# Accumulations of the first layer's two GEMMs emitted in four pieces each, with attention steps between the pieces; front order searched anew

## The chip, the cores and the metric

The program runs on one core of one Trainium2 chip. Its time is the device time of one execution in microseconds (us); of several runs the median counts. The engines are TensorE (PE: matmuls and transposes; PEld is its weight load), VectorE (DVE), ScalarE (ACT), GpSimd (POOL) and SyncE (SP, which here only issues DMAs). Each engine works through its instructions in the order in which the kernel emits them, and an instruction waits until what it reads is written and what it overwrites is read.

## What is computed

```python
# attention: q, k, v are (2, 8, 576, 64); heads 0-3 see the last 32 positions,
# heads 4-7 every fourth of the last 128
scores = where(mask, q @ k.T / 8, -1e9);  attn = softmax(scores);  a = attn @ v
x = a.transpose(0, 2, 1, 3).reshape(1152, 512)
# first layer (moe_*, w_in 512 x 1024, w_out 1024 x 512)
h = x @ w_in;  solu = h * softmax(h)
ln = (solu - mean(solu)) / sqrt(var(solu) + 1e-6) * g_ln
x = ln @ w_out
# second layer (moe2_*, four experts, w1 512 x 1024, w2 1024 x 512)
out = sum_e p[:, e] * (relu(x @ w1[e]) @ w2[e])
```

The first layer's weights come as float64 and are turned into float32 on the chip, by bit operations. Every GEMM is done in three products of rounded halves (high by high, high by low, low by high), so each operand is first split into a high and a low part.

## The kernel before

The front of the kernel (attention and the first layer) and the first eighth of the second layer are written as generators, each a chain of short steps, and the string ORDER says in which order the steps are emitted. A name in ORDER means the next step of that generator; the loop at the end of `fused_kernel` calls `next` on it. A plus behind a name sets `alt`, which moves that step's work to another engine: a copy (`copy`) from ACT to DVE, an addition or subtraction (`pick`) from DVE to POOL, or the other way round for `poolv`. A star and a number behind a name would set `fill`, the number of extra bf16 matmuls that `busy` emits; no entry has a star. As each engine keeps the emitted order, a step that waits holds up what stands behind it on its engine, and nothing else.

The names, in which b is the batch half and t a third of its 576 positions:

- `lI.j`, `lO.j.t`, `lD.u.b`, `lP.t.b`, `lvd.b`, `lvp.t.b`, `lW.g`, `lV.g`: loads, all on SP's queue. lP and lD bring q and k of the plain and the dilated heads, lI w_in, lO w_out, lvp and lvd v, lW and lV the second layer's weights.
- `AP.t.b`, `AD.u.b`: q, then k are transposed on PE into a PSUM pair and copied to SBUF; steps 1 and 3 are PE's, 2 and 4 the copies.
- `UP.t.b`, `UD.t.b`: one of twelve attention units in twelve steps: scores on PE (1), maximum, subtraction (DVE: 2, 3), exponential (ACT: 4), sum, reciprocal (DVE: 5, 6), product (DVE, or POOL with a plus: 7), transposes (PE: 8), copy (9), values (PE: 10), high part (11) and low part (12) of x.
- `VI.j`: w_in's rows 128 j and on, in seven steps: two on ACT, two on DVE, an addition, the high part, the low part; j = 0 and 4 are the two halves of the first 128 rows. `VO.j.t`: w_out's rows 256 j + 128 t and on, also seven steps, scaled by g_ln.
- `H.t`: the first GEMM for 128 positions. Its 24 matmuls (four k blocks, three products, two halves of the 1024 columns) go into one PSUM pair `pm`; then maximum (DVE), exponential (ACT), product with h and its sum (DVE), centring (DVE or ACT).
- `T.t`: eight transposes of H.t's result, its square's sum (ACT), high and low part.
- `X.c.dp`: the second GEMM for 384 positions and half of the output columns, 48 matmuls into one pair `pm`, then one copy. X.c needs T of three tiles.
- `WP.g`, `WV.g`, `XQ.s`: operands of the second layer (weights and x; its products follow a scheme with seven instead of eight block products); `u.s` and `d.t` are its two GEMMs for the first group g = 0. `endE`, `endA`, `endH`, `endX` free memory, `misc` and `sc` are small.

H.t needs the attention units that cover its positions: of the plain heads (k blocks 0 and 1) those of its 192 positions, of the dilated heads (k blocks 2 and 3) two or three units, since these run over every fourth position. So H.0 needs UP.0.0, UD.0.0 and UD.1.0, and H.1 needs UP.0.0, UP.1.0 and all three UD of the first half.

There are two PSUM pairs under the name `pm` and two under `pa`. `pm` serves AD, the first half's AP, H, X and every second product of the second layer; `pa` serves the rest. A step that takes a pair waits until the last reader of the pair two before it is done: for H that is the product's step, for X the copy.

A step of H, as it is emitted (L380 to L388):

```python
for kk in range(KD):
    ...
    for i, (xx, ww, n) in enumerate(seq):
        nc.tensor.matmul(pm[:, n, :], ...)
yield
```

From the second group of the second layer on (g = 1 to 7, from 260 us) plain loops set the order.

Of the kernel before, what the change touches and what calls it, by code (L numbers as in the profile page):

```python
# [21 lines left out]
ORDER = """
lI.0 VI.0 lI.3 VI.0 lP.0.0 lD.1.0 AP.0.0 AP.0.0 VI.0 AD.1.0 VI.3 VI.3 lI.4 VI.3 AP.0.0 VI.3 VI.4 VI.4 lD.0.0 VI.3 AP.0.0 lP.1.0 lI.1 UP.0.0 AD.1.0
VI.3+ AD.1.0 UP.0.0 AD.0.0 AD.1.0 VI.4 AD.0.0 AD.0.0 UP.0.0 AP.1.0 AD.0.0 UP.0.0 lD.0.1 VI.0 VI.3+ AP.1.0 lvp.0.0 lI.2 UD.0.0 AP.1.0 UD.1.0 lvd.0 VI.4
VI.4 VI.0+ UD.0.0 UD.0.0 UD.0.0 UD.2.0 UD.1.0 VI.1 VI.0 UP.0.0 UD.1.0 UP.0.0 lP.2.0 UD.2.0 UD.0.0 UD.0.0 UP.0.0+ VI.0+ UP.0.0 VI.4 UD.1.0 UD.0.0+ VI.1
lO.0.1 UD.1.0 AP.1.0 UD.2.0 UD.1.0 UP.0.0 VI.1 UP.0.0 UD.2.0 VI.1 UD.1.0+ UD.2.0 UP.0.0+ UP.0.0 VI.2 UD.0.0 UD.0.0+ AD.0.1 UP.1.0 UD.1.0 VI.4+ UP.1.0
AD.0.1+ VI.2 lO.0.0 lP.0.1 UD.2.0 VI.2 UP.1.0 UD.0.0 UD.1.0 VI.2 AD.0.1 lvp.1.0 VI.2 lD.1.1 UD.0.0 VI.1+ UD.1.0 VI.1 AD.0.1+ UP.1.0 UD.1.0 VI.2 VI.1+
UP.1.0 UD.1.0 VO.0.0 VI.2 VO.0.1 AP.2.0 VO.0.0 UD.2.0+ UD.0.0 AP.2.0 H.0 UP.1.0 UP.1.0+ H.0 VO.0.0 AP.2.0 VO.0.1 UP.1.0 UD.2.0 VO.0.0 H.0 UP.1.0 misc
UD.2.0 UP.1.0 AP.0.1 H.0 VO.0.0+ UP.1.0+ AD.1.1 UP.1.0 VO.0.1 AP.2.0 AP.0.1 VO.0.1 UP.2.0 UP.2.0 VO.0.1+ lO.1.0 UD.2.0 AD.1.1 UD.2.0 lvp.2.0 AD.1.1
UP.2.0 endE lP.1.1 UD.2.0 VO.0.0 AD.1.1 VO.1.0 VO.0.0 UP.2.0 VO.1.0 H.0 VO.0.1 H.1 UP.2.0 VO.1.0 VO.1.0 UP.2.0 VO.1.0 AP.0.1 H.1 AP.0.1 UP.2.0+ T.0  # L30
UP.2.0 VO.0.1 H.1 T.0 T.0+ lO.1.1 H.1 T.0 lO.2.0 H.1 VO.1.1 VO.1.1 UP.2.0 H.2 AP.1.1 VO.1.1 UP.2.0 VO.1.1 VO.2.0 H.2 VO.1.1+ AP.1.1 UP.2.0 UP.2.0 H.2
UD.0.1 UD.0.1 VO.1.0 UP.0.1 UD.0.1 UP.0.1 VO.1.0 UD.0.1 UD.0.1 UD.0.1 lO.2.1 H.2 UD.0.1+ T.1 T.1 UP.0.1 VO.1.1 VO.2.0 VO.2.0 lvd.1 H.3 VO.2.1 VO.1.1
lvp.0.1 T.1 VO.2.0 VO.2.1 T.1 AP.1.1 VO.2.1 UP.0.1 VO.2.1 UD.0.1 AP.1.1 UD.1.1 UP.0.1 UP.0.1 UD.1.1 UD.0.1 VO.2.0+ VO.2.0 UD.0.1 UD.0.1 UD.1.1 UD.0.1
lP.2.1 AP.2.1 UD.1.1 lO.3.0 UP.0.1+ AP.2.1 lvp.2.1 UP.0.1 UD.1.1 H.2 UD.2.1 UP.0.1 UD.1.1 UP.0.1 UD.1.1+ UD.2.1 UD.2.1 UP.0.1 VO.2.1+ UP.0.1 AP.2.1
AP.2.1+ UD.1.1 VO.3.0 UD.2.1 UD.1.1 T.2 UD.1.1 lO.3.1 H.3 VO.2.1 UD.1.1 UD.2.1 T.2 UD.2.1 VO.2.0 VO.2.1 UD.1.1 T.2+ H.4 VO.3.1 T.2 VO.3.0 VO.3.1 VO.3.0
UD.2.1+ VO.3.1 VO.3.0 UP.1.1 UP.1.1 VO.3.0+ UD.2.1 H.3 UD.2.1 UP.1.1 VO.3.0 UP.2.1 H.3 VO.3.1 UP.1.1 UP.1.1 VO.3.1 VO.3.0 VO.3.1 VO.3.1 UD.2.1 UD.2.1
H.3+ UP.1.1 X.0.1 UP.1.1+ UP.2.1 UP.2.1 lvp.1.1 UP.1.1 H.4 UP.2.1 UP.2.1 UP.2.1 H.4 UD.2.1 UP.2.1 UP.2.1 H.4 UP.1.1+ UP.1.1 UP.2.1 UP.2.1 UP.2.1 endA
UP.1.1 X.0.1 X.0.0 H.5 UP.1.1 X.0.0+ T.3 T.3 H.5 T.3 H.6 H.5 H.4+ UP.2.1 T.4 T.4 H.5 H.6 T.3 T.4+ H.6 H.5 H.7 H.6 T.5 T.5 H.8 H.7 H.7 H.6+ T.4 H.7 T.6
# [715 lines left out]
```

## Time and profile before

| | us |
|---|---|
| median of three runs | 561.86 (561.75 to 563.1) |
| the profiled execution | 561.9 |
| its span | 560.1 |
| PE busy | 533.2 (95%) |
| DVE busy | 365.1 (65%) |
| ACT busy | 197.5 (35%) |
| POOL busy | 191.6 (34%) |

The span runs from the first to the last instruction of one profiled execution. An engine's busy time is the time in which it has an instruction in work; neighbouring instructions of one engine can overlap by some tens of ns, so the sum of their durations can be a little more than the busy time. The rest is idle time; where the profile knows what ended a wait, it names it behind an arrow.

### The profile page before, as it was taken

To read this page: it belongs to the slowest core of one execution; us is meant where nothing else is said; L and a number is where in the kernel's file an instruction comes from. 1 tells how busy PE (TensorE), PEld (TensorE's weight loads), DVE (VectorE), ACT (ScalarE), POOL (GpSimd) and SP (SyncE) were. 2 spreads that over 40 slices of the span, in tenths; PEclk is the share of its full clock that TensorE was granted. 3 is DMA by queue.
4 is the path that set the end of the run, shared out by engine and by line. 5 is a ranking of instruction groups with operands and counts; after the bars stand their busy time and mean duration, and the time that the engine had idled before them with its cause. 6 is when DMAs were issued, how large, how long until landed. Compare 5 with 4: busy or idle time off the path is not lost.

```text
span 560.1 us, 9023 instructions
## 1 busy us (share of the span) xinstructions
PE 533.2 (95%) x3772; PEld 479.6 (86%) x3772; DVE 365.1 (65%) x472; ACT 197.5 (35%) x309; POOL 191.6 (34%) x143
## 2 busy tenths in 40 slices
...
DMA packets 33944, 35.79 MB, mean 64 GB/s; under 512 B 18800, under 2 KB 21872, under 8 KB 33520
## 3 DMA queue, kind: packets, MB, share of 16 engines
...
q14 instruction: 11, 0.09, 0.1%
...
## 4 chain that ended last, share of the span: by engine, by line
PE 84%; DVE 8%; ACT 3%; issue 2%; DMA 1%; SPq 1%; DVEq 0%; ACTq 0%
PE pa L615 18%; PE pm L615 17%; PE pm L545 15%; PE pa L545 15%; PE pm L386 9%; PE pm L433 6%; PE pa L357 2%; DMA draw<-in_moe_w_in_dram 1%; PE pa L413 1%; DVE xol L464 1%; PE pa L343 1%; PE pa L318 1%; DVE hl L464 1%; ACT pt L184 1%; DVE cva L206 1%
## 5 line engine op out<-in xcount | busy, mean ns | idle before, releaser
L558 DVE SCALAR_TENSOR_TENSOR hl<-ct,hh 128x512 fp32r<-128x512 f32 (+1 forms) x64 | 63.2, 1005 | 33.3 <-ACT hh L556 33.2
L556 ACT ACTIVATE hh<-ct 128x512 fp32r<-128x512 f32 (+1 forms) x64 | 42.2, 682 | 59.7 <-DVE ct L588 29.7
L545 PE MATMUL pm<-xoh,hh 128*128 128x256 f32 (+1 forms) x192 | 56.9, 296 | 1.1 <-DVE ct L588 1.1
L615 PE MATMUL pm<-wh,hh 128*128 128x512 f32 (+1 forms) x148 | 56.9, 384 | 0.6 <-DVE xf L620 0.6
L545 PE MATMUL pm<-xol,hh 128*128 128x256 f32 (+1 forms) x192 | 56.9, 297 | 0.3 <-DVE xol L464 0.3
L545 PE MATMUL pa<-xoh,hh 128*128 128x256 f32 (+1 forms) x192 | 56.9, 296 | 0.0
L545 PE MATMUL pa<-xoh,hl 128*128 128x256 f32 (+1 forms) x192 | 56.8, 296 | 0.0
L545 PE MATMUL pm<-xoh,hl 128*128 128x256 f32 (+1 forms) x192 | 56.8, 296 | 0.0
L545 PE MATMUL pa<-xol,hh 128*128 128x256 f32 (+1 forms) x192 | 56.8, 296 | 0.0
L615 PE MATMUL pm<-wl,hh 128*128 128x512 f32 (+1 forms) x148 | 56.8, 384 | 0.0
L615 PE MATMUL pm<-wh,hl 128*128 128x512 f32 (+1 forms) x148 | 56.7, 383 | 0.0
L615 PE MATMUL pa<-wh,hh 128*128 128x512 f32 x144 | 56.2, 390 | 0.1
L615 PE MATMUL pa<-wl,hh 128*128 128x512 f32 x144 | 56.1, 390 | 0.0
L615 PE MATMUL pa<-wh,hl 128*128 128x512 f32 x144 | 56.0, 389 | 0.0
L464 POOL TENSOR_TENSOR wl<-wl,wh 128x1024 fp32r<-128x1024 f32 x8 | 19.3, 2412 | 96.6 <-ACT wh L184 95.4
L620 DVE SCALAR_TENSOR_TENSOR xf<-pm,pr,xf 128x512 f32<-128x512 f32 (+1 forms) x33 | 24.1, 730 | 32.9 <-PE pm L615 32.9
L620 DVE SCALAR_TENSOR_TENSOR xf<-pa,pr,xf 128x512 f32<-128x512 f32 x31 | 23.1, 745 | 29.4 <-PE pa L615 29.4
L184 ACT CAST wh<-wl 128x1024 fp32r<-128x1024 f32 x15 | 15.8, 1053 | 71.0 <-PE pa L615 40.6
L464 POOL TENSOR_TENSOR hl<-sw,hh 128x512 fp32r<-128x512 f32 x20 | 30.4, 1520 | 27.8 <-ACT hh L184 27.8
L545 PEld LDWEIGHTS pm<-xoh,hh 128*128 128x128 f32 x192 | 36.4, 190 | 1.6 <-issue 1.3
L572 POOL TENSOR_TENSOR ct<-ct,ct 128x512 f32<-128x512 f32 (+1 forms) x15 | 22.3, 1484 | 45.0 <-ACT ct L570 45.0
L545 PEld LDWEIGHTS pm<-xol,hh 128*128 128x128 f32 x192 | 36.4, 190 | 0.8 <-DVE xol L464 0.5
...
## 6 DMA issues: line engine op xcount, KB each, us to landing
...
```

The costliest lines, as they stand in the source:

```text
L184: nc.scalar.copy(out, in_)
L206: pick().tensor_tensor(out=au, in0=au, in1=low.bitcast(U32), op=ALU.add)
L357: nc.tensor.matmul(po[64 * row:64 * row + 64, 0, o:o + 96], lhsT=vv, rhs=pt[:, j, :, g, :], start=True, stop=True)
L386: nc.tensor.matmul(pm[:, n, :], lhsT=xx[:, kk, cols], rhs=ww["in", kk][:, 512 * n:512 * n + 512], start=(kk == 0 and i < 2), stop=(kk == K ...
L433: nc.tensor.matmul(pm[:, dd, 0:CW], lhsT=w_, rhs=x_[:, f, :], start=(f == 0 and i == 0), stop=(f == KF - 1 and i == 2))
L464: pick().tensor_tensor(out=out, in0=a, in1=b, op=op)
L545: nc.tensor.matmul(ps[:, ff, 0:n], lhsT=a[:, kk, fc], rhs=b[:, kk, :], start=kk == 0 and m == 0, stop=kk == 1 and m == 2)
L556: nc.scalar.activation(out=hv, in_=src, func=AF.Relu)
L558: nc.vector.scalar_tensor_tensor(out=lv, in0=src, scalar=0.0, in1=hv.bitcast(F32), op0=ALU.max, op1=ALU.subtract)
L572: poolv().tensor_tensor(out=c12, in0=c21, in1=c22, op=ALU.add)
L615: nc.tensor.matmul(po[:, u, 0:dn], lhsT=h_[:, f, cols], rhs=w_, start=(f == 0 and i == 0), stop=(f == 3 and i == 2))
L620: nc.vector.scalar_tensor_tensor(out=acc[:, t, dc], in0=po[:, u, 0:dn], scalar=pr[:, t, e:e + 1], in1=acc[:, t, dc], op0=ALU.mult, op1=ALU ...
```

## The change

H.t yields after each of its four k blocks, and X.c.dp after each pair of f blocks, with both halves of its output columns in turn; so each is emitted in four pieces of 6 or 12 matmuls, and ORDER names an H eight times instead of five and an X five times instead of twice. The number of matmuls and the operands are the same. `KORD` is the order of H's k blocks, which is as before. The tile `warmb`, `busy`, `fill` and the four calls of `busy` are gone.

ORDER is new as a whole. It differs from the old one in the sequence of steps and in which steps have a plus. Of the additions and subtractions in the front, the old order gives POOL 11 of 12 products of attention, 4 of 5 low parts of w_in and 2 of 5 additions there, and 6 of 8 additions for w_out; the new one 7, 1, 3 and 7. The old order's head and the new order's head, its part around the end of attention and its part around the start of the second layer:

```diff
 ORDER = """
-lI.0 VI.0 lI.3 VI.0 lP.0.0 lD.1.0 AP.0.0 AP.0.0 VI.0 AD.1.0 VI.3 VI.3 lI.4 VI.3 AP.0.0 VI.3 VI.4 VI.4 lD.0.0 VI.3 AP.0.0 lP.1.0 lI.1 UP.0.0 AD.1.0
-VI.3+ AD.1.0 UP.0.0 AD.0.0 AD.1.0 VI.4 AD.0.0 AD.0.0 UP.0.0 AP.1.0 AD.0.0 UP.0.0 lD.0.1 VI.0 VI.3+ AP.1.0 lvp.0.0 lI.2 UD.0.0 AP.1.0 UD.1.0 lvd.0 VI.4
-VI.4 VI.0+ UD.0.0 UD.0.0 UD.0.0 UD.2.0 UD.1.0 VI.1 VI.0 UP.0.0 UD.1.0 UP.0.0 lP.2.0 UD.2.0 UD.0.0 UD.0.0 UP.0.0+ VI.0+ UP.0.0 VI.4 UD.1.0 UD.0.0+ VI.1
-lO.0.1 UD.1.0 AP.1.0 UD.2.0 UD.1.0 UP.0.0 VI.1 UP.0.0 UD.2.0 VI.1 UD.1.0+ UD.2.0 UP.0.0+ UP.0.0 VI.2 UD.0.0 UD.0.0+ AD.0.1 UP.1.0 UD.1.0 VI.4+ UP.1.0
-AD.0.1+ VI.2 lO.0.0 lP.0.1 UD.2.0 VI.2 UP.1.0 UD.0.0 UD.1.0 VI.2 AD.0.1 lvp.1.0 VI.2 lD.1.1 UD.0.0 VI.1+ UD.1.0 VI.1 AD.0.1+ UP.1.0 UD.1.0 VI.2 VI.1+
-UP.1.0 UD.1.0 VO.0.0 VI.2 VO.0.1 AP.2.0 VO.0.0 UD.2.0+ UD.0.0 AP.2.0 H.0 UP.1.0 UP.1.0+ H.0 VO.0.0 AP.2.0 VO.0.1 UP.1.0 UD.2.0 VO.0.0 H.0 UP.1.0 misc
-UD.2.0 UP.1.0 AP.0.1 H.0 VO.0.0+ UP.1.0+ AD.1.1 UP.1.0 VO.0.1 AP.2.0 AP.0.1 VO.0.1 UP.2.0 UP.2.0 VO.0.1+ lO.1.0 UD.2.0 AD.1.1 UD.2.0 lvp.2.0 AD.1.1
-...
+lP.0.0 AP.0.0 lI.0 VI.0 AP.0.0+ AP.0.0 VI.0 lI.3 AP.0.0+ UP.0.0 lD.1.0 VI.3 VI.3 lD.0.0 VI.3 AD.1.0 UP.0.0 lI.4 UP.0.0 VI.0 lP.1.0 AD.0.0 lI.1 AD.1.0
+lI.2 VI.3 AD.1.0 VI.3 VI.3 AD.1.0 AD.0.0+ VI.4 VI.4 AD.0.0 VI.0 lP.2.0 AD.0.0+ VI.3 VI.4 VI.4 VI.0+ AP.1.0 UD.0.0 VI.0+ lvp.0.0 lD.0.1 AP.1.0 UP.0.0
+VI.4+ UD.0.0 UD.1.0 VI.4 UD.0.0 UD.0.0 UP.0.0 UD.0.0 UD.0.0 lvd.0 VI.1 VI.1 UD.0.0+ UD.1.0 UD.2.0 lO.0.0 UD.1.0 VI.4 AP.1.0 UD.2.0 VI.1 misc AP.1.0
+UP.0.0 VI.1 VI.2 UD.0.0 UD.1.0 UD.2.0 VI.0 VI.2 UP.0.0 UP.0.0 UD.1.0 UD.0.0 UD.1.0 lvp.1.0 UP.0.0 UP.1.0 AP.2.0 UP.0.0 UD.1.0 VI.1 VI.1 VI.2 AD.0.1
+UP.0.0 lD.1.1 VI.2 AP.2.0 UP.1.0 UP.1.0 lO.0.1 AD.0.1 UP.0.0 AP.2.0 UD.1.0 UP.1.0 lP.0.1 VI.2+ AD.0.1 UP.1.0 UD.0.0 AP.2.0+ H.0 UD.1.0 VI.2 VI.2+
+UD.2.0 UD.0.0+ UD.0.0 UD.1.0 VI.1 UP.1.0 UD.1.0+ UD.2.0 UD.1.0 UP.2.0 H.0 H.0 AD.0.1 VO.0.0 UD.2.0 UD.2.0 VO.0.0 UP.2.0 H.0 UP.1.0+ UP.2.0 UP.2.0
+UP.1.0 VO.0.0 H.0 UD.2.0 UP.1.0 UP.1.0 H.0 VO.0.0 UP.1.0+ UD.2.0 AD.1.1 H.0 AD.1.1 UP.2.0 VO.0.1 UP.1.0 lP.1.1 UD.2.0 AD.1.1 endE VO.0.1 UD.2.0+ H.1
+UD.2.0 H.0 UP.2.0 AD.1.1 H.1 VO.0.0+ UP.2.0+ VO.0.1 AP.0.1 VO.0.0 VO.0.1 T.0 AP.0.1 VO.0.0 T.0 T.0 VO.0.1+ UD.0.1 UD.0.1 UD.0.1 T.0 VO.0.1 H.1 H.1
+...
+UP.1.1 UP.2.1 VO.2.0+ VO.2.1 X.0.1 H.4 VO.2.1 H.4 VO.2.1 lvp.2.1 UP.1.1 H.4 UP.1.1 lO.3.0 VO.3.0 UP.2.1 UD.2.1 UD.2.1+ VO.2.0 VO.2.0 UP.1.1 VO.2.1+
+UP.2.1 lO.3.1 VO.2.1 VO.2.1 VO.3.1 VO.3.1 X.0.1 UP.1.1 UP.1.1 X.0.0 UP.1.1 VO.3.1 UD.2.1 VO.3.0 VO.3.1 X.0.0 X.0.1 VO.3.0 VO.3.0 UP.2.1 VO.3.0+ UD.2.1
+UP.2.1 VO.3.1 lvp.1.1 X.0.0 UD.2.1 VO.3.0 VO.3.1 VO.3.0 UP.1.1 VO.3.1 UP.2.1 H.3 X.0.1 UP.1.1+ UP.2.1+ UP.1.1 UP.2.1 UP.1.1+ endA X.0.1 X.0.0 UP.1.1
+H.5 X.0.0+ H.6 H.5 T.3 T.3 H.5 H.4 H.5 H.5 H.5 H.6 T.3+ T.4 H.5 T.3 T.4 H.6 H.6 H.7 H.7 H.7 H.5 T.5 H.6 H.6 H.6 T.4 T.5 H.6+ H.7 H.8 H.7 H.8 H.7 H.8
+T.4 T.6 T.5 H.7 H.7+ T.6 T.5 H.8 H.8 T.6+ X.1.1 H.8 X.1.1 H.8 X.1.0 X.1.1 H.8 T.6 T.7 T.8 T.8 T.7 X.1.1 X.1.1+ X.1.0 X.1.0 X.1.0 T.7 endH T.7 lW.0
+WP.0+ T.8 T.8 X.2.0 WP.0 sc WP.0 X.1.0 WP.0 WP.0+ WP.0 WP.0 WP.0 XQ.0 X.2.1 XQ.0 WP.0 X.2.0 WP.0 XQ.0 XQ.0 XQ.0+ WP.0+ X.2.0 WP.0 XQ.0 X.2.0 X.2.1
+XQ.0+ X.2.1 XQ.0 X.2.0 X.2.1 XQ.0+ WP.0 XQ.0 XQ.0 endX XQ.0+ XQ.0 WP.0+ XQ.0+ WP.0 WP.0+ XQ.1+ X.2.1+ WP.0 XQ.0 XQ.1 WP.0+ XQ.0 XQ.1 u.0 u.0 XQ.1 u.0
+...
 """
```

The rest of the diff:

```diff
+KORD = (0, 1, 2, 3)
-    warmb = ap1.tile([128, 224], BF16, name="warmb", tag="warmb")
-    nc.vector.memset(warmb, 0.0)
 ...
-    fill = [0]
-    def busy(ps):
-        for _ in range(fill[0]):
-            nc.tensor.matmul(ps[:, 1, 288:512], lhsT=warmb[:, 0:128], rhs=warmb, start=True, stop=True)
 ...
-            busy(pa)
 ...
-            busy(pa)
 ...
-        busy(ps)
 ...
-        busy(po)
 ...
     def moe_H(t):
         pm = psm.tile([128, 2, 512], F32, name="pm", tag="pm")
         cols = slice(128 * t, 128 * t + 128)
-        for kk in range(KD):
+        for n_, kk in enumerate(KORD):
             seq = [(xhi, whi, n) for n in range(2)] + [(xhi, wlo, n) for n in range(2)] + [(xlo, whi, n) for n in range(2)]
             for i, (xx, ww, n) in enumerate(seq):
                 nc.tensor.matmul(pm[:, n, :], lhsT=xx[:, kk, cols], rhs=ww["in", kk][:, 512 * n:512 * n + 512],
-                                 start=(kk == 0 and i < 2), stop=(kk == KD - 1 and i >= 4))
-        yield
+                                 start=(n_ == 0 and i < 2), stop=(n_ == KD - 1 and i >= 4))
+            yield
         e = ep.tile([128, 2, 512], F32, name="e", tag="e")
         nc.vector.tensor_reduce(out=nmx[:, t:t + 1], in_=pm, axis=AX.XY, op=ALU.max, negate=True)
         yield
 ...
     def moe_X(c, dp):
         lh, ll = hts["ln", c]
         pm = psm.tile([128, 2, 512], F32, name="pm", tag="pm")
-        for dd in range(2):
-            d = 2 * dp + dd
-            for f in range(KF):
-                o = (f % 2) * 512 + d * 128
-                wh = whi["out", f // 2][:, o:o + 128]
-                wl = wlo["out", f // 2][:, o:o + 128]
-                for i, (w_, x_) in enumerate(((wh, lh), (wh, ll), (wl, lh))):
-                    nc.tensor.matmul(pm[:, dd, 0:CW], lhsT=w_, rhs=x_[:, f, :], start=(f == 0 and i == 0), stop=(f == KF - 1 and i == 2))
-        yield
+        for j in range(KF // 2):
+            for f in (2 * j, 2 * j + 1):
+                for dd in range(2):
+                    d = 2 * dp + dd
+                    o = (f % 2) * 512 + d * 128
+                    wh = whi["out", j][:, o:o + 128]
+                    wl = wlo["out", j][:, o:o + 128]
+                    for i, (w_, x_) in enumerate(((wh, lh), (wh, ll), (wl, lh))):
+                        nc.tensor.matmul(pm[:, dd, 0:CW], lhsT=w_, rhs=x_[:, f, :], start=(f == 0 and i == 0), stop=(f == KF - 1 and i == 2))
+            yield
         copy(xf[0].rearrange("p (k n) -> p k n", k=KD)[:, 2 * dp:2 * dp + 2, c * CW:c * CW + CW], pm[:, :, 0:CW])
     xf = []
 ...
-        fill[0] = int(n or 0)
```

## Rows read from the trace of the kernel before

**Rows 1.** the page's head and engine part (busy us, share, instructions)

```profile
span 560.1 us, 9023 instructions
...
PE 533.2 (95%) x3772; PEld 479.6 (86%) x3772; DVE 365.1 (65%) x472; ACT 197.5 (35%) x309; POOL 191.6 (34%) x143
```

**Rows 2.** stretches of the span: length, then each engine's busy time (x instructions)

```profile
12.34:39.68 27.34, 21.04 (x370) 16.70 (x369) 24.98 (x37) 16.36 (x26) 13.58 (x10) 1.00 0.96 259
39.68:53.12 13.44, 11.74 (x143) 9.88 (x144) 10.17 (x17) 8.70 (x15) 6.66 (x5) 1.00 0.38 75
53.12:70.30 17.18, 16.77 (x195) 13.94 (x194) 15.17 (x23) 11.82 (x22) 2.54 (x3) 1.00 0.43 123
70.30:96.86 26.56, 23.86 (x360) 19.13 (x357) 23.60 (x42) 18.33 (x32) 7.71 (x8) 1.00 0.47 110
96.86:108.72 11.86, 11.46 (x95) 11.08 (x93) 9.24 (x19) 4.92 (x7) 0.83 (x1) 1.00 0.00 1
108.72:177.50 68.78, 68.78 (x385) 64.71 (x385) 40.11 (x50) 23.95 (x38) 12.22 (x7) 1.00 0.05 16
...
190.00:210.00 20.00, 18.17 (x98) 15.52 (x97) 17.50 (x21) 7.22 (x12) 9.62 (x6) 1.00 0.23 80
```

**Rows 3.** PE's timeline: start, duration, instructions, idle time before and what ended it

```profile
8.87 0.88 PE L288 MATMUL pm<-ident,rpq 96*128 96x96 f32 x4 [8.87 <-DMA rpq<-in_q_dram]
...
39.68 0.73 PE L386 MATMUL pm<-wh,xhi 128*128 128x512 f32 x2 [0.69 <-DVE kTd L182]
...
52.92 0.71 PE L386 MATMUL pm<-wh,xhi 128*128 128x512 f32 x2
...
76.19 0.82 PE L343 MATMUL pa<-ident,pd 128*128 128x128 f32 x6
```

**Rows 4.** DVE's groups by shape, 0 to 205 us: count | busy, mean ns

```profile
L390 DVE TENSOR_REDUCE nmx<-pm 128x1 f32<-128x1024 f32 x9 | 11.0, 1222 | 10.0 <-PE pm L386 10.0
...
L256 DVE TENSOR_TENSOR xlo<-pa,xhi 128x384 fp32r<-128x384 f32 x10 | 6.7, 670 | 3.7 <-ACT xhi L184 3.6
...
L326 DVE TENSOR_REDUCE st<-pa 128x6 f32<-128x384 f32 x12 | 6.6, 551 | 3.2 <-PE pa L318 3.1
...
L106 DVE MEMSET sm<- 128x6 f32 x3 | 0.1, 63 | 0.0
```

**Rows 5.** timeline of all engines, around the first wide conversion of w_in

```profile
10.17 1.12 ACT L198 ACTIVATE draw<-draw 128x1024 int32<-128x1024 uint32 x1
...
12.34 0.69 DVE L202 TENSOR_SCALAR eva<-eva 128x1024 uint32<-128x1024 uint32 x1 [5.42 <-ACT eva L200]
```

**Rows 6.** stretches of the start; DMA share and GB/s stand last

```profile
0.00:2.00 2.00, 0.00 (x0) 0.00 (x0) 0.99 (x6) 1.28 (x1) 1.33 (x8) 1.00 0.09 20
...
6.00:7.00 1.00, 0.00 (x0) 0.00 (x0) 0.43 (x1) 0.47 (x1) 0.53 (x5) 1.00 0.98 365
7.00:8.00 1.00, 0.00 (x0) 0.00 (x0) 0.00 (x0) 0.00 (x0) 0.00 (x0) 1.00 1.18 272
8.00:9.00 1.00, 0.13 (x1) 0.16 (x2) 0.00 (x0) 0.00 (x0) 0.00 (x0) 1.00 1.16 334
```

**Rows 7.** the chain of work that ended last: start, us, what

```profile
45.45 1.24 DVE nmx L390
...
46.71 1.21 ACT e L392 x2
...
96.93 8.55 PE pm L433 x48
...
117.25 5.49 PE pm L386 x24
...
142.60 8.35 PE pm L433 x48
...
189.22 2.45 DVE ct L584
```

**Rows 8.** the loads of w_in (tile draw), issue to landing

```profile
DMA to landing us min/median/max: 6.9/8.6/10.4
```

23 lines of the change are left out of this document (8 added, 15 removed).

## The prediction

> **What bounds the kernel now.** I read the profiled execution first: its span is 560.1 us and PE (TensorE) is busy for 533.2 of it [rows 1]. So at most 26.9 us of PE idle time can be won; the change removes no matmul. The view by stretches says where those lie [rows 2]: 6.3 us between 12.34 and 39.68 (21.04 busy of 27.34), 1.7 to 53.12, 0.4 to 70.30, 2.7 to 96.86, 0.4 to 108.72, nothing at all from there to 177.50, and 1.8 between 190 and 210. Before 12.34 PE has 9.8 us of idle time, because its first instruction, the transposes of the first q load, starts at 8.87 when that load lands [rows 3]. So the second layer's loop after 210 us is not in question, and the time is decided by how late PE is when the front ends.
>
> What holds PE back in the front is VectorE (DVE). In the stretch from 12.34 to 39.68 it is busy 24.98 of 27.34 us, 91%, and from 53 to 97 us 88 to 89% [rows 2]. The first group of the first GEMM (H.0) starts at 39.68 and waits for DVE until then [rows 3]. A check by counting, each emitted step at the mean of its kind in the view of DVE's groups (83 rows; the first, the last and two that are used most are shown [rows 4]): the steps ahead of H.0 in the old order hold 27.6 us of DVE work, 0.4 of it done before 12.34; 12.34 + 27.2 = 39.5, against 39.68 measured. Rows of neighbouring DVE steps overlap a little: up to the end of attention I count 87.4 us after 12.34, while the stretches show 83.2 busy to 108.72 and about 0.2 less without endA's steps and with the last xlo. So counted DVE work is worth 0.95 of its sum (83.0 / 87.4), at a busy share of 86.3% over 12.34 to 108.72 (83.2 of 96.4).
>
> **The change part by part.** *The warm-up tile and its calls.* No entry of the order has a star, so no warm-up matmul ran before. What goes is one short memset at DVE's start, ahead of 5.4 us in which it waits anyway [rows 5]: 0.
>
> *Pieces.* H keeps its 24 matmuls and X its 48; only where they stand changes. X now alternates its two PSUM halves after every three matmuls. H alternates after each one, and takes 5.49 / 24 = 229 ns for 512 columns, against 8.35 / 48 = 174 ns for 384 in X [rows 7]; per column H is not dearer, so alternation costs 0. A group that follows attention steps takes a little longer than one behind another group: X 8.55 against 8.35 [rows 7]. The new order has some 12 more such joints ahead of the end of attention. At 0 to 0.2 us each this is 0 to 2.4; half of it stands where PE would wait for DVE anyway, and I take 0.8.
>
> *The first loads.* The load lP.0.0 (q and k for the first plain unit) goes from third place in SP's queue to first, ahead of lI.0 and lI.3 (w_in). DVE's long work starts with lI.3's conversion. Before, this was at 12.34, 2.17 us after ACT began on it at 10.17 [rows 5]; ACT had first to serve the q transposes of 8.87 [rows 3], so it was the q load that was late, not lI.3. In the new order lP.0.0, lI.0 and lI.3 are 0.39 + 0.52 + 1.05 = 1.97 MB. The DMA engines had moved 1.88 MB by 8.0 us and 2.22 by 9.0 (eight rows from 0 to 9 us, first and last shown [rows 6]), so 1.97 are through at 8.25. A load is seen some 1.25 us after its bytes: the old q load's 1.77 MB mark is passed at 7.6, and PE starts at 8.87. Thus lI.3 lands at 9.5 and DVE can start on it at 11.7, 0.6 earlier, with two copies of lP.0.0 (0.55 each) already done. The bounds: not earlier than 8.3; not later than 13.3, which is an issue near 2.9 plus 10.4, the longest w_in load [rows 8]. The loads behind change places too: lI.2 passes lD.0.1 and lvp.0.0, and lP.2.0 goes ahead of lvd.0, so 8.1 MB have to move until lvd.0 is in, not 7.7; at 259 GB/s [rows 2] that is 31 us. Its first reader is UD.0.0's last matmul group, behind 26.5 us of counted DVE work, at about 37: hidden, and 0.4 MB more would stay hidden.
>
> The Trainium skill (DMA: Bandwidth & Descriptors, Specifications) wants 512 B for a transfer at line rate, and lP.0.0 reads runs of 256 B; the trace agrees, with 365 GB/s while w_in alone was moving and 272 when the q load came [rows 6]. By that rule the whole of 1.97 MB at 272 GB/s from 2 us on would be through at 9.2 and lI.3 seen at 10.5, and the sum would be 560.9.
>
> *DVE work ahead of H.1.* H.1's first piece needs UP.0.0 and UP.1.0 complete. The new order emits 40.1 us of counted DVE work up to that: w_in's five conversions 15.2, eighteen attention steps at 0.55 [rows 4] 10.0, their split into high and low part 5.2 (low 0.67 [rows 4]), short attention steps 2.7, copies of transposes 3.1, H.0's two reductions 2.5, w_out 1.3. Less the two early copies 39.0, times 0.95 = 37.1. At 91%, DVE's share in the first stretch, that is 40.6 us: H.1 starts at 11.7 + 40.6 = 52.3; at 86.2%, its share from 12.34 to 53.12 (35.15 of 40.78 [rows 2]), at 54.7. The low share before came from the wait for H.0's 5.5 us block; in pieces DVE has attention steps at hand, so I take 90%: 52.9. Before, H.1 started at 52.92 [rows 3] with one AP step (0.5 us) more done on PE. So here the change gives -0.5 (between +0.2 and -2.3, and 1 us more for each us that lI.3 lands later).
>
> *From H.1 to the end of attention.* The old order has 3.5 us of PE idle time left here (0.4 + 2.7 + 0.4 [rows 2]). The largest part ends at X.0.1, which waited for all eight chunks of w_out, 81.1 us of counted DVE work against 69.8 us of PE work ahead of it: 11.3 more. PE work is counted in the same way, from its timeline between 45 and 97 us: per attention unit scores 1.0, transposes 0.8 [rows 3] and values 0.87, 0.67 or 0.49 per q or k transposed, a T 0.87, an H 5.46, an X 8.35 [rows 7]; ahead of X.0.1 in the old order 12, 10 and 10 of the first three (28.7), 5.4 + 5.9 of transposes, three T and five H. In pieces X needs chunk pair j only for piece j, so the last of VO.2.1 and both halves of VO.3 stand behind the first piece, and X.0.1's gate is 75.5 against 68.2: 7.3 more. Four us of DVE delay can therefore be absorbed that could not before. H.1's gate, 40.1 against 28.1 (12.0), is the tightest of the new order; after it none exceeds 10.7, most are 6 to 9. Against that stand 7.0 us more DVE work by the end of attention (94.8 counted against 87.8): fewer steps go to POOL (24.1 counted there, 31.1 before). I take 1.3 us of idle time left of the 3.5, a gain of 2.2 (between 3.5 and -2.8, the latter below).
>
> *From there to the second layer.* Behind endA both orders have the same PE work to go (H.5 starts after 89.9 us of PE work in both), and PE had no idle time here [rows 2]. H.5 to H.8 in pieces keep two PSUM pairs open, and X.1.0 needs H.8's: H.8's last piece ends 4.2 us of PE work ahead of it, its maximum and exponential take 1.24 + 1.21 [rows 7], and a product as long follows. That is just hidden; bounds 0 to 1.5, I take 0. X.2.1's pair waits for a copy behind lW.0's first conversion on ACT; the slot is 2.1 us, both together 1.4. The 1.8 us between 190 and 210 came from a chain in which one DVE addition (L584) took 2.45 us [rows 7]; the new order gives that one to POOL and a shorter-lived one to DVE. I take a gain of 1.1, between 1.8 and -1.
>
> **Sum.** -0.5 + 2.2 - 0.8 + 1.1 = 2.0 us gained. The profiled execution took 561.9 for its span of 560.1, the median of three runs is 561.86, so they are the same to 0.1: 561.86 - 2.0 = 559.9.
>
> **The rivals.** (1) *DVE sets the end* (slower). The 7 us moved from POOL lie on the engine that paces the front. The last gate of attention (UP.1.1's last matmuls) needs 93.0 counted us of DVE work, less 1.1, times 0.95 = 87.3, with 87.0 of PE work ahead. If the waits on DVE come from the chains themselves (softmax steps that go to ACT and back) and not from long blocks, its share stays or falls. At 83% it is 11.7 + 105.2 = 116.9, PE is 29.9 late; before it was 27.1 late at X.0.1 (96.9 [rows 7] - 69.8): 2.8 slower, 564.7. Level is at 85.3%, and 0.3% slower at 83.9%. For it: 88 to 89% is all that DVE reached between 53 and 97 us. Against: even the old 86.3% gives 25.9, a gain of 1.2. Chance 0.17.
>
> (2) *lI.3 lands late* (slower): at its latest, 13.3, H.1 starts 3.8 later; all the rest as forecast, 1.8 slower, 563.7. Level from 11.5 on. Against: the bytes. Chance 0.06.
>
> (3) *No change*: the gates loosen, but joints at 0.2 us and the waits for ACT's copies that pieces don't touch keep 2 to 3 of the 3.5 us: 561.5. Chance 0.25.
>
> (4) *All of it*: no idle time after H.1, the chain at 190 gone, H.1 at 52.3: 0.2 + 3.5 + 1.8 - 0.4 = 5.1 faster, 556.8. Chance 0.14.
>
> (5) *The forecast*, 558.3 to 561.0: 0.38.
>
> **How the numbers follow.** A measurement of this kernel tells about 0.3%, 1.7 us, from no change. Faster by more: two thirds of (5), all of (4), a little of (3): 0.44. Within: the rest of (5), most of (3), a part of (1) and (2): 0.33. Slower: 0.23. The range leaves out the far halves of (4) and (1): 556.3 to 563.9.
>
> **What would show it.** DVE's first wide shift (lI.3) at about 11.7; H.1's first piece near 53; PE's idle time from there to the end of attention near 1.3 us instead of 3.5; DVE's share up to it above 87%; u.0 without a wait of 1 us. The prediction is wrong if H.1 starts after 55 or DVE's share falls under 85%, or if PE shows new waits for PSUM pairs behind endA.

## The result: slower by 3.5 us, and the profile after

The changed kernel takes 565.35 us (median of five runs, 564.75 to 566.5), the kernel before 561.9: a ratio of 1.0062 [1.0044, 1.008]. Measured again later, in one group with the experiments: 565.0, a ratio of 1.0052 [1.0035, 1.0069]. 559.9 was forecast. The profiled execution took 565.35 for a span of 563.6.

The page's head, PE's busy time and the row of granted clock (tenths of full speed in 40 slices), against [rows 1]:

```profile
span 563.6 us, 9028 instructions
...
PE 534.3 (95%) x3772; PEld 477.7 (85%) x3772; DVE 370.5 (66%) x477; ACT 196.1 (35%) x304; POOL 188.6 (33%) x142
...
PEclk9969999999999999999999999999999999999999
```

PE's idle time rose from 26.9 to 29.3 us, DVE's work by 5.4 us. The stretches say where (length, then PE, PEld, DVE, ACT, POOL busy; granted clock, DMA share, GB/s):

```profile
14.17:54.74 40.57, 30.43 (x456) 24.07 (x457) 35.44 (x60) 23.22 (x36) 10.64 (x8) 0.87 0.88 193
54.74:108.72 53.98, 53.98 (x635) 45.84 (x633) 45.30 (x77) 35.72 (x62) 12.89 (x12) 1.00 0.36 99
...
176.40:186.40 10.00, 8.61 (x67) 8.00 (x66) 9.72 (x14) 2.86 (x4) 1.47 (x1) 1.00 0.89 311
186.40:196.40 10.00, 9.06 (x66) 8.80 (x65) 9.30 (x12) 4.61 (x7) 4.27 (x2) 1.00 0.20 52
196.40:206.40 10.00, 8.78 (x43) 7.16 (x43) 8.72 (x8) 2.27 (x5) 7.31 (x4) 1.00 0.19 52
206.40:216.40 10.00, 8.49 (x46) 7.24 (x45) 10.00 (x12) 3.91 (x7) 8.20 (x6) 1.00 0.01 2
```

From H.1 to the end of attention PE has no idle time left where [rows 2] had 3.5 us. But in the 40 us behind u.0's first product it is idle 5.06 us (the last four of these stretches); before, in the 40 us behind the same product, 1.83:

```profile
177.50:217.50 40.00, 38.17 (x249) 35.09 (x248) 36.84 (x45) 16.83 (x27) 19.16 (x11) 1.00 0.33 106
```

PE's timeline at four places (start, duration, instructions, and in brackets the idle time before and what ended it), against [rows 3]:

```profile
41.73 0.73 PE L377 MATMUL pm<-wh,xhi 128*128 128x512 f32 x2
...
54.74 0.71 PE L377 MATMUL pm<-wh,xhi 128*128 128x512 f32 x2
...
176.36 0.28 PE L537 MATMUL pa<-xoh,hh 128*128 128x256 f32 x1
...
182.07 0.38 PE L537 MATMUL pm<-xoh,hh 128*128 128x256 f32 x1 [1.24 <-DVE xf L177]
...
194.95 0.41 PE L537 MATMUL pa<-xoh,hh 128*128 128x320 f32 x1 [0.94 <-DVE ct L586]
198.20 0.50 PE L607 MATMUL pa<-wh,hh 128*128 128x512 f32 x1 [1.23 <-DVE ct L558]
...
210.17 0.41 PE L537 MATMUL pa<-xoh,hh 128*128 128x320 f32 x1 [1.51 <-DVE xf L610]
```

H.0 is 2.1 us later than before and H.1 1.8; u.0's first product (L537) is 1.1 us earlier, at 176.36 against 177.5 (where X.2's last stretch ends in [rows 2]). From there to the end it is 387.2 us against 382.6. So the front gained 1.1 us in this execution, and the second layer lost 4.6. The stretch from u.0 to the end, in the kernel before and in the changed one:

```profile
177.50:560.10 382.60, 377.06 (x2221) 341.89 (x2220) 237.41 (x273) 108.38 (x166) 143.08 (x88) 1.00 0.14 48
...
176.36:563.60 387.24, 378.00 (x2221) 341.83 (x2220) 241.94 (x273) 107.13 (x164) 147.51 (x91) 1.00 0.14 47
```

Of the 4.6 us, 3.7 are idle time of PE (9.24 against 5.54) and 0.9 busy time (378.00 against 377.06).

The first of the four waits is new in kind: u.0's fourth product, its second on a pair `pm` (an expectation below calls it the second product), takes the pair of X.2.1 and waits for X.2.1's copy. DVE's timeline shows what stood ahead of that copy:

```profile
170.99 2.32 DVE L456 TENSOR_TENSOR xol<-xf,xoh 128x1024 fp32r<-128x1024 f32 x1
173.23 1.51 DVE L177 CAST xoh<-ct 128x512 fp32r<-128x512 f32 x1
174.78 1.94 DVE L456 TENSOR_TENSOR xol<-ct,xoh 128x512 fp32r<-128x512 f32 x1
176.64 1.51 DVE L177 CAST xoh<-ct 128x512 fp32r<-128x512 f32 x1
178.19 0.69 DVE L456 TENSOR_TENSOR xol<-ct,xoh 128x512 fp32r<-128x512 f32 x1
...
180.00 0.42 DVE L177 CAST xoh<-xf 128x512 fp32r<-128x512 f32 x1
180.45 0.69 DVE L456 TENSOR_TENSOR xol<-xf,xoh 128x512 fp32r<-128x512 f32 x1
181.06 0.95 DVE L177 COPY xf<-pm 128x768 f32<-128x768 f32 x1
```

DVE goes without a gap from 170.99 to 182.0, for the most part through XQ.0's operations. X.2.1's last matmul started at 176.19, but its copy, which a plus has put on DVE, came at 181.06. Meanwhile ACT, which has such copies where there is no plus, sat idle for 8.90 us, and POOL was at work until 177.9. ACT's timeline, then POOL's:

```profile
182.10 1.27 ACT L179 CAST xoh<-xf 128x1280 fp32r<-128x1280 f32 x1 [8.90 <-DVE xf L177]
```

```profile
170.55 1.68 POOL L456 TENSOR_TENSOR ct<-xf,ct 128x512 f32<-128x512 f32 x1 [3.02 <-DVE ct L456]
172.24 2.23 POOL L456 TENSOR_TENSOR hl<-sw,hh 128x512 fp32r<-128x512 f32 x1
174.42 1.75 POOL L456 TENSOR_TENSOR sw<-xf 128x640 f32<-128x640 f32 x1
176.13 1.74 POOL L456 TENSOR_TENSOR hl<-rw,hh 128x512 fp32r<-128x512 f32 x1
```

At the start, ACT's and DVE's first work on lI.3 (timeline, against [rows 5]):

```profile
11.98 1.15 ACT L193 ACTIVATE draw<-draw 128x1024 int32<-128x1024 uint32 x1 [3.05 <-DMA draw<-in_moe_w_in_dram]
...
14.17 0.69 DVE L197 TENSOR_SCALAR eva<-eva 128x1024 uint32<-128x1024 uint32 x1 [6.68 <-ACT eva L195]
```

Four of w_in's five loads, those of one line, from issue to landing ([rows 8] has 6.9, 8.6 and 10.4; the fifth, lI.4, took 13.5 here), and three stretches with their GB/s at the end (against [rows 6]):

```profile
DMA to landing us min/median/max: 9.1/10.5/12.0
```

```profile
8.00:9.00 1.00, 0.51 (x34) 0.27 (x16) 0.00 (x0) 0.93 (x2) 0.00 (x0) 1.00 0.94 373
9.00:10.00 1.00, 0.00 (x0) 0.00 (x0) 0.00 (x0) 0.00 (x0) 0.00 (x0) 1.00 1.10 248
10.00:11.00 1.00, 0.00 (x0) 0.00 (x0) 0.00 (x0) 0.00 (x0) 0.00 (x0) 1.00 1.06 221
```

lI.3 was seen by ACT at 11.98 and reached DVE at 14.17.

### The profile page after: what moved, and what is told of

Read it like the earlier page. It is cut to its first block, busy times and chain, and to the rows that moved or that the text cites. A ratio compares the mean times of both kernels' runs of the same rounds, so it can differ in the third digit from the quotient of the medians.

```text
span 563.6 us, 9028 instructions
## 1 busy us (share of the span) xinstructions
PE 534.3 (95%) x3772; PEld 477.7 (85%) x3772; DVE 370.5 (66%) x477; ACT 196.1 (35%) x304; POOL 188.6 (33%) x142
## 4 chain that ended last, share of the span: by engine, by line
PE 81%; DVE 11%; DMA 2%; ACT 2%; issue 2%; SPq 0%; POOL 0%; POOLq 0%; DVEq 0%
PE pm L607 17%; PE pa L607 16%; PE pa L537 14%; PE pm L537 14%; PE pm L377 9%; PE pm L425 5%; DVE xol L456 2%; DMA draw<-in_moe_w_in_dram 2%; PE pa L348 2%; PE pa L335 1%; PE pa L404 1%; DVE hl L550 1%; PE pa L310 1%; DVE xoh L177 1%; DMA rw<-in_moe_w_dram 1%
## 5 line engine op out<-in xcount | busy, mean ns | idle before, releaser
L550 DVE SCALAR_TENSOR_TENSOR hl<-ct,hh 128x512 fp32r<-128x512 f32 (+1 forms) x64 | 64.8, 1032 | 35.1 <-ACT hh L548 35.1
L537 PE MATMUL pa<-xoh,hh 128*128 128x256 f32 (+1 forms) x192 | 57.1, 297 | 2.9 <-DVE xf L610 1.5
L537 PE MATMUL pm<-xoh,hh 128*128 128x256 f32 (+1 forms) x192 | 57.0, 297 | 1.2 <-DVE xf L177 1.2
L537 PE MATMUL pa<-xoh,hl 128*128 128x256 f32 (+1 forms) x192 | 56.8, 296 | 0.0
L537 PE MATMUL pm<-xoh,hl 128*128 128x256 f32 (+1 forms) x192 | 56.8, 296 | 0.0
L537 PE MATMUL pa<-xol,hh 128*128 128x256 f32 (+1 forms) x192 | 56.8, 296 | 0.0
L537 PE MATMUL pm<-xol,hh 128*128 128x256 f32 (+1 forms) x192 | 56.8, 296 | 0.0
L456 POOL TENSOR_TENSOR wl<-wl,wh 128x1024 fp32r<-128x1024 f32 x7 | 16.9, 2413 | 95.7 <-ACT wh L179 95.7
L456 POOL TENSOR_TENSOR hl<-sw,hh 128x512 fp32r<-128x512 f32 x22 | 33.9, 1544 | 28.3 <-ACT hh L179 28.3
L537 PEld LDWEIGHTS pa<-xoh,hh 128*128 128x128 f32 x192 | 36.4, 190 | 4.2 <-DVE xf L610 1.9
L537 PEld LDWEIGHTS pm<-xoh,hh 128*128 128x128 f32 x192 | 36.4, 190 | 2.0 <-DVE xf L177 1.4
L537 PEld LDWEIGHTS pm<-xol,hh 128*128 128x128 f32 x192 | 36.4, 190 | 0.3
```

The lines of the kernel that those rows point to most:

```text
L456: pick().tensor_tensor(out=out, in0=a, in1=b, op=op)
L537: nc.tensor.matmul(ps[:, ff, 0:n], lhsT=a[:, kk, fc], rhs=b[:, kk, :], start=kk == 0 and m == 0, stop=kk == 1 and m == 2)
L550: nc.vector.scalar_tensor_tensor(out=lv, in0=src, scalar=0.0, in1=hv.bitcast(F32), op0=ALU.max, op1=ALU.subtract)
```

## The experiments

Two columns of this table come from each profiled execution: the start of u.0's first product, and the time from there to the end of the span. The first varies among executions of the same front: of eight profiles with the changed kernel's first loads seven have 175.1 to 176.9 and one, that of s_casts, 180.9; that execution was the longest of its twelve (566.81 us; the median is 562.4). The second hardly varies within a kernel (387.2 and 387.3 for the changed one), so it prices the second layer's start apart from the front's variation. It is not free of the front, though: e3_both has 384.0, and p_joined, with the same sequence of steps behind a front 29 us longer, 382.4, probably because DVE has more of its work done where PE reaches u.0 late. Times are medians, ratios are to the kernel before on the same chip, whose medians were 562.3 to 562.5.

| kernel | u.0 at | u.0 to end | time | ratio |
|---|---|---|---|---|
| before | 177.5 | 382.6 | 562.49 | 1 |
| changed, again | 175.4 | 387.3 | 565.0 | 1.0052 [1.0035, 1.0069] |
| e1_old_second | 175.2 | 384.0 | 561.85 | 0.9997 [0.9981, 1.0013] |
| e2_loads_first | 173.6 | 387.2 | 563.81 | 1.0023 [1.001, 1.0037] |
| e3_both | 175.4 | 384.0 | 560.2 | 0.9957 [0.9945, 0.997] |
| e4_before_new_second | 178.3 | 384.0 | 563.43 | 1.0017 [1.0008, 1.0025] |
| s_pre | 176.6 | 384.8 | 563.25 | 1.0022 [1.0009, 1.0036] |
| s_marks | 175.1 | 384.4 | 561.97 | 1.0002 [0.9984, 1.002] |
| s_x21 | 175.4 | 385.5 | 562.91 | 1.0017 [1.0004, 1.0031] |
| s_casts | 180.9 | 384.1 | 562.4 | 1.0006 [0.9988, 1.0024] |
| s_nopool | 176.9 | 385.2 | 562.86 | 1.0007 [0.9994, 1.002] |
| m_before | 177.3 | 384.0 | 563.2 | 1.002 [1.0011, 1.0028] |
| b_marks_loads | 176.3 | 384.4 | 560.86 | 0.9979 [0.9965, 0.9994] |
| b_all | 176.6 | 382.6 | 560.84 | 0.9965 [0.9951, 0.9979] |
| p_joined | 204.7 | 382.4 | 589.54 | 1.0479 [1.0459, 1.05] |
| p_before_pieces | 196.6 | 382.4 | 581.89 | 1.0347 [1.0333, 1.0362] |

**Front or second layer.** e1_old_second has the changed kernel's order up to the end of T.8 and the old sequence behind it (of ORDER, here and below, only stretches that differ are shown):

```diff
-endH T.7 lW.0 WP.0+ T.8 T.8 X.2.0 WP.0 sc WP.0 X.1.0 WP.0 WP.0+
+endH T.7 lW.0 T.8 T.8 sc X.1.0 XQ.0 WP.0+ WP.0+ WP.0 WP.0+ XQ.0
```

> The changed kernel (median 565.35 us) with its order of steps kept to the end of T.8, and from there the steps of the second layer's start (XQ, WP, X.2, u.0, u.1, d.0 to d.3) in the sequence of the kernel before; X.2.0 and X.2.1 issue their four pieces where that sequence had their one. Theory A (the loss lies in the order of the second layer's start: TensorE sat idle 5.06 us in the 40 us after u.0's first product, 1.83 us before): that idle time goes back to about 1.8 us, and the time falls by about 3.2 us, to 562.1 (561.2 to 563.2). Theory B (the loss comes from the late first loads and the late H.1, and the idle time in u.0 only follows from it): u.0's idle time stays near 5 us and the time within 1 us of 565.35. Theory C (the lower granted clock between 25 and 39 us): no change either, 565.35.

Theory A: 561.85, 3.1 us faster than the changed kernel beside it. u.0 to the end falls to 384.0 and PE's idle time in the 40 us behind u.0's start to 3.08; theory A had 1.8. So 3.2 of the 4.6 us go, and 1.4 stay with the old sequence behind the new front.

e2_loads_first puts two loads back in front, e3_both does both:

```diff
-lP.0.0 AP.0.0 lI.0 VI.0 AP.0.0+ AP.0.0 VI.0 lI.3 AP.0.0+
+lI.0 lI.3 lP.0.0 AP.0.0 VI.0 AP.0.0+ AP.0.0 VI.0 AP.0.0+
```

> The changed kernel with the two loads lI.0 and lI.3 issued ahead of lP.0.0 again, as the kernel before had them, all else in the changed order. In the changed kernel the wide shift of lI.3 started at 14.17 us (12.34 before) and H.1 at 54.74 (52.92 before), and TensorE was busy without a gap from H.1 to the last product of X.2. Theory B (DVE's first weight work gates H.1, and nothing takes up a shift of H.1 any more): the shift starts 1.5 to 2 us sooner, H.1 1.0 to 2.0 us sooner, and the time falls by as much, to 563.9 (563.3 to 564.4). Theory A (nothing before u.0 matters to the loss): H.1 moves, but the time stays within 0.5 us of 565.35 because DVE, not TensorE, sets when u.0 may run. Rival D (the q and k loads behind 2 MB land later, and AP.0.0 at the head of TensorE's and DVE's queues holds all up): H.1 0 to 2 us later, 565.4 to 567.4.

> Both edits together: lI.0 and lI.3 first, and the second layer's start in the sequence of the kernel before. Theories A and B together (two losses that add up): 565.35 - 3.2 - 1.4 = 560.7 (559.7 to 562), below the kernel before (561.9). A alone: 562.1; B alone: 563.9. If DVE sets the end of the front, with the loads' gain spent waiting for it: 562.

The wide shift of lI.3 moved from 14.17 (13.24 in the second profile of the changed kernel) to 11.43 us, H.1 from 54.74 (53.81) to 51.92. The time fell by 1.2 us, and by 1.65 from e1 to e3. By the times theory B holds beside A: the two losses add, and e3_both beats both kernels, by 2.3 us against the one before. That the gain goes through H.1 is shown in this one profile only: in e3_both, b_marks_loads and b_all, which issue the loads in the same way, the shift starts at 11.6 to 12.0 us, but H.1 at 53.8 to 55.0.

> The kernel before (561.9 us) with the second layer's start alone in the new sequence (its steps after T.8, X.1.0 and sc; each X.2 product is issued whole where its first piece stands in the new order). Theory A (the new sequence of these steps is itself the loss): TensorE's idle time after u.0's first product rises from 1.83 to about 5 us and the time to 565.1 (564 to 566). Theory B (the sequence does harm only because the front before it ends otherwise): the time stays within 1 us of 561.9.

Here the expected number failed: 0.9 us slower, not 3. u.0 to the end takes 384.0, 1.4 more than before: waits of 1.5 and 1.2 us are there, the wait of 1.24 us for X.2.1's copy is not. DVE comes to that copy through the same operations as in the changed kernel, but 2.2 us behind u.0's first product (180.49 against 178.28), not 4.7. So that wait needs the changed sequence together with the changed front.

**Which steps of the second layer.** c_after repeats the changed kernel; s_pre has e1_old_second's sequence up to u.0 and the changed one from there; s_marks moves no step and takes four pluses off. s_pre at the joint (against e1_old_second), then s_marks (against the changed kernel):

```diff
-u.0 X.2.1 u.0 XQ.1 XQ.1 u.0 u.0 XQ.1 u.0 WV.0 u.0 WP.0+
+u.0 X.2.1 u.0 WP.0+ XQ.1 XQ.1 XQ.1 u.0 u.0 u.0 XQ.1 u.0
```

```diff
-XQ.0 XQ.0+ WP.0+
+XQ.0 XQ.0 WP.0+
...
-X.2.1 XQ.0+ X.2.1
+X.2.1 XQ.0 X.2.1
...
-endX XQ.0+ XQ.0
+endX XQ.0 XQ.0
...
-XQ.1+ X.2.1+ WP.0
+XQ.1+ X.2.1 WP.0
```

> The changed kernel itself once more, beside the others of this group and the kernel before on the same chip, as their base. All theories: 565.4 (564.8 to 566.5), 2.5 to 3.7 us above the kernel before.

> The changed kernel with the sequence of the kernel before only between endH and u.0 (XQ.0, WP.0, the rest of X.2), and from u.0 on the changed sequence. The whole tail put back gave 3.5 us. Theory M (the loss begins in XQ.0's steps and the rest follows): 562 (561.3 to 563). Theory L (two parts, ahead of u.0 and behind it): the first wait of 1.24 us goes, the later ones, 3.7 us against 1.8 us in the kernel before, stay: 564.0 (563.4 to 564.6).

> The changed kernel with four pluses taken off: the second, third and fifth of XQ.0's six casts and X.2.1's copy run on ACT instead of DVE; no step moves. In the changed kernel DVE worked without a gap from 170.99 to 182.1 us on XQ.0's operations, 4.4 us of them these four, while ACT sat idle 8.90 us before 182.10 and TensorE waited 1.24 us for X.2.1's copy. Theory M (these four are the first cause, and the three later waits of 0.94, 1.23 and 1.51 us follow from DVE's lateness): all of the loss returns, 3.2 us, to 562.2 (561.5 to 563.2). Theory L (each of the later waits has its own cause in the order of u.1 and d): only the first wait goes, 1.24 us, to 564.1 (563.6 to 564.7). If DVE's queue is not what X.2.1's copy waits for: 565.4.

Three casts and a copy moved from DVE to ACT give back 3.0 us, all of the loss against the kernel before. In s_marks X.2.1's copy starts at once, on ACT, and the wait of 1.24 us is gone; the waits of 1.5 and 1.2 stay, 0.94 becomes 0.7. ACT's timeline, then PE's waits from 175 to 215 us (total, times, longest):

```profile
175.27 0.80 ACT L179 COPY xf<-pm 128x768 f32<-128x768 f32 x1 [2.21 <-PE pm L425]
```

```profile
PE pa L537 <- DVE xf L610: 1.5, 1, 1.5
PE pa L607 <- DVE ct L558: 1.2, 1, 1.2
PE pa L537 <- DVE ct L586: 0.7, 1, 0.7
```

s_pre, with a gain of 1.75 us, lies between the theories. Theory M named the right place but not the way: the later waits did not follow from the first, they stayed, and the gain is larger than the waits that went: from u.0 to the end 2.8 us, of which 1.0 is PE's busy time (376.96 against 378.00).

To part the copy from the three casts, s_x21 has only the last of the four edits above, s_casts only the first three:

> The changed kernel (565.0 us) with one plus taken off: X.2.1's copy alone goes to ACT, which sat idle for 8.90 us there; the three casts of XQ.0 stay on DVE. Theory C (the copy's place at the back of DVE's queue is the loss; all four marks gave 3.0 us): it gives most of it, 562.0 to 563.2. Theory F (DVE's load is the loss: 0.95 us of the 4.4 us go): 0.7 us, 564.0 to 564.8.

> The changed kernel with the pluses of the three casts of XQ.0 taken off and X.2.1's copy left on DVE. Theory C: the copy still stands last in DVE's queue, but that queue is 3.4 us shorter (1.51 + 1.51 + 0.42 us), so that it comes before u.0's second product wants its pair: 563.5 to 564.3 at the worst, 562.0 if the queue was all. Theory F (load): 3.4 of 4.4 us of DVE's time back, 562.3 to 563.0.

The copy alone gives 2.1 us, the casts alone 2.6, together 3.0. Either way X.2.1's copy comes in time, by leaving the queue or by a shorter queue ahead of it, and what the second edit adds to the first is small. s_x21 fits theory C and not F. s_casts, at 562.4, lies in F's range and near the lower of C's two values, so it does not part them. DVE's load counts beside the copy's place: with the copy alone on ACT, DVE is still late, and u.0's sixth product waits for its addition (L558); with the casts alone on ACT neither of these two waits is there. PE's timeline of s_x21:

```profile
183.67 0.39 PE L537 MATMUL pm<-xoh,hh 128*128 128x256 f32 x1 [0.94 <-DVE ct L558]
```

**POOL beside DVE.** s_nopool takes the pluses off the four operations of POOL shown above (one of XQ.0, two of WP.0, the first of XQ.1), so that DVE does more:

```diff
-WP.0+ XQ.0+ WP.0 WP.0+ XQ.1+ X.2.1+ WP.0 XQ.0 XQ.1 WP.0+
+WP.0+ XQ.0 WP.0 WP.0 XQ.1 X.2.1+ WP.0 XQ.0 XQ.1 WP.0
```

> The changed kernel with four other pluses taken off, those of the four additions and subtractions that POOL did from 170.55 to 177.9 us beside XQ.0's work on DVE, so that DVE does them (0.69 to 0.82 us each, 2.9 us). In the changed kernel DVE's rows beside them were longer than the same rows alone: two casts 1.51 us against 0.42, one subtraction 1.94 against 0.69. Theory P (POOL's work beside it slows DVE's, so POOL's help there saves nothing): DVE's rows fall back to their short times, 3.4 us and more, X.2.1's copy comes 0.5 to 1 us sooner and the time is 564.0 to 565.0. Theory Q (POOL's help counts in full): X.2.1's copy up to 2.9 us later, 566 to 568.

DVE has 2.9 us more to do, and the kernel is 2.1 us faster: theory P, with a larger gain than its 564.0 to 565.0. The same DVE operations as above, in s_nopool's timeline, with POOL idle:

```profile
171.61 1.22 DVE L456 TENSOR_TENSOR xol<-xf,xoh 128x1024 fp32r<-128x1024 f32 x1
172.75 0.42 DVE L177 CAST xoh<-ct 128x512 fp32r<-128x512 f32 x1
173.20 0.69 DVE L456 TENSOR_TENSOR xol<-ct,xoh 128x512 fp32r<-128x512 f32 x1
173.81 0.42 DVE L177 CAST xoh<-ct 128x512 fp32r<-128x512 f32 x1
...
179.08 0.95 DVE L177 COPY xf<-pm 128x768 f32<-128x768 f32 x1
```

2.32 became 1.22, 1.51 became 0.42 twice, 1.94 became 0.69: 4.5 us back for 2.9 added (2.2 of the 2.9 ahead of the copy). X.2.1's copy starts 2.2 us after u.0's first product (at 176.9) instead of 4.7. The Trainium skill (SBUF — State Buffer, Who interferes with whom) says that DVE and GpSimd share one pair of ports, held by one of them for a whole instruction, and that DVE's casts can want it, and its operations with two SBUF inputs where GpSimd reads SBUF; these rows agree.

**The mirror.** m_before adds pluses to the kernel before, on XQ.0's second, third and fifth cast and on X.2.1's copy:

```diff
-XQ.0+ XQ.0 XQ.0 WP.0+ XQ.0 WP.0
+XQ.0+ XQ.0+ XQ.0 WP.0+ XQ.0+ WP.0
...
-WP.0 XQ.0 XQ.0 XQ.0 X.2.0+
+WP.0 XQ.0 XQ.0+ XQ.0 X.2.0+
...
-u.0 X.2.1 u.0
+u.0 X.2.1+ u.0
```

> The mirror: the kernel before with four pluses added, on three of XQ.0's casts that ran on ACT (the second, third and fifth) and on X.2.1's copy, so that they run on DVE; no step moves. Theory M (DVE is full there, and any cast moved from ACT to it delays the second layer's start): 2.5 to 3.5 us slower than the kernel before, 565 to 566. Theory M' (it costs only where the copy of X.2.1 stands last in that queue, as the changed order put it; here u.0's first product and two copies of slack lie between): 562.5 to 563.5.

0.9 us slower, u.0 to the end 384.0: theory M'. In the old order the copy, on DVE, starts at 180.78, 3.5 us behind u.0's first product, and no PE wait for it appears; what is new is a wait of 0.9 us for a DVE addition (L581).

**The repairs together.** b_marks_loads joins the edits of s_marks and e2_loads_first, b_all those of s_nopool too.

> The changed kernel with the four pluses taken off and the two loads lI.0 and lI.3 issued first: the two repairs together, everything else as changed. The four marks alone gave 565.0 - 562.0 = 3.0 us, the loads alone 565.0 - 563.8 = 1.2 us. If the two losses add: 560.8 (560 to 561.6), under the kernel before (562.5) by 1.7 us. If DVE's load in the second layer's start takes up what the front gains: 562.

> The changed kernel with all repairs: loads lI.0 and lI.3 first, the four pluses off (XQ.0's casts and X.2.1's copy on ACT) and the four of POOL's additions on DVE. Loads and four marks gave 560.9; POOL's four alone gave 565.0 - 562.9 = 2.1 us. If the two ways of freeing DVE add: 558.8. If they take away the same wait (X.2.1's copy late in DVE's queue): 560.9 (560.2 to 561.5). If the additions now load DVE where ACT's casts had made room: 561.5 to 563.

Loads and marks add, to 560.86. The four operations taken from POOL give nothing more in the median (560.84). But u.0 to the end falls by another 1.8 us, to 382.6, as in the kernel before; the wait for X.2.1's copy was gone already, and of the three waits that the marks had left (1.5, 1.2 and 0.7) two are there, in the 40 us behind u.0's first product:

```profile
PE pa L537 <- DVE xf L610: 1.5, 1, 1.5
PE pa L607 <- DVE ct L558: 0.7, 1, 0.7
```

The times of the two kernels spread over 4 us each, in twelve and eleven executions, so whether the two ways of freeing DVE add is open: the medians say no, the profiles yes. With u.0 to the end as in the kernel before, what is left of the change is its front: 1.6 us between b_all's median and that of the kernel before beside it (562.4).

**The pieces by themselves.** p_joined is e3_both with each accumulation whole again, in its fourth piece's place; p_before_pieces is the kernel before with H in four pieces, spread over at most 16 steps and ahead of the reduction. Their edits in `moe_H`:

```diff
 def moe_H(t):
+    yield; yield; yield
     pm = psm.tile(...)
     for n_, kk in enumerate(KORD):
         ...
-        yield
+    yield
```

```diff
     for kk in range(KD):
         ...
-    yield
+        yield
```

> The version with the loads first and the second layer's start put back (560.2 us), with the four pieces of every H and X accumulation issued together where the fourth piece stood; steps and order unchanged. Theory P (the pieces are what removed TensorE's idle time between H.1 and the second layer, 3.5 us before and none after): idle time of 2 to 5 us comes back there and the time rises to 563.5 (562 to 566). Theory S (the new order alone removed it, and whole accumulations would have done): within 0.7 us of 560.2.

> The kernel before in its old order, with each H accumulation issued in four pieces: the first where the whole stood, the other three spread over the steps up to the reduction that reads it (over 16 steps at most); X stays whole, nothing else moves. Theory P (the pieces fill TensorE's waits in attention, 3.5 us between H.1 and the end of attention): idle time there falls to 1 to 2.5 us and the time to 560.5 to 561.8. Theory S (without a new order the waits stay: DVE's and ACT's results come when they come, and the first products of each GEMM only move apart): 562 to 563. Rival: later ends of H delay the exponentials and T behind them: 563 to 565.

Neither theory foresaw 29 and 20 us more. u.0's first product comes 19.1 us later in p_before_pieces than in the kernel before; 14.2 of these are idle time of PE. The waits for T's operands, which the whole products had covered (0.2 us in all), lie open (PE's timeline), beside a new one of 2.48 us in attention:

```profile
65.25 0.55 PE L288 MATMUL pa<-ident,rpq 96*128 96x96 f32 x4 [2.48 <-ACT pt L184]
...
132.36 1.09 PE L413 MATMUL pa<-ident,e 128*128 128x128 f32 x8 [0.93 <-ACT e L397]
140.45 1.09 PE L413 MATMUL pa<-ident,e 128*128 128x128 f32 x8 [1.52 <-DVE e L399]
149.31 1.97 PE L413 MATMUL pa<-ident,e 128*128 128x128 f32 x8 [2.29 <-ACT e L397]
...
168.87 1.94 PE L413 MATMUL pa<-ident,e 128*128 128x128 f32 x8 [5.02 <-DVE esum L644]
```

A piece that is moved behind a T no longer hides that T's wait. So pieces spread in this way through the old order cost 20 us, and the new order with whole accumulations at the fourth piece's place 29; other spreads and other places were not run. What the pieces alone bring cannot be read from these two runs.

## Why the prediction was wrong, step by step

- **From there to the second layer: the step that failed.** It took "a gain of 1.1, between 1.8 and -1", "u.0 without a wait of 1 us", and what came was -4.6 (u.0 to the end 387.2 against 382.6). It looked at one DVE addition (L584) and at the pair that X.2.1 takes, and not at the pair that X.2.1 gives back, which u.0's fourth product wants, nor at what stands ahead of that copy in DVE's queue. That was in reach: the new order has X.2.1+ behind six of XQ.0's steps, and [rows 2] show DVE busy 17.5 of 20 us a little later, from 190 to 210. The 5.7 us between forecast and measurement of this term are the whole miss of 5.45. Four waits make 3.2 of the 4.6 (5.06 less 1.83), one of 0.45 us between 400 and 450 us, also gone in s_marks, belongs to it too; the last 0.9 is PE's busy time, also gone in s_marks, and what makes it longer stays open.
- **The first loads: wrong.** lI.3 was to land at 9.5 and to reach DVE at 11.7; ACT saw it at 11.98, and it came to DVE at 14.17 (12.66 to 14.62 in seven more profiles with these first loads). The landing kept within its bounds, 8.3 to 13.3, but lies behind the 11.5 from which rival (2) had no gain left. The step counted bytes as if they landed in the order of issue. 2.0 MB were through at 9.0 us, 0.75 later than counted, but lI.3 was seen only at 11.98, with 2.7 MB through: loads issued behind it must have had their share. Rival (2) was right in kind; it cost 1.1 to 1.65 us by three pairs of runs.
- **DVE work ahead of H.1: right by luck.** From DVE's start to H.1 it took 40.57 us, 41.2 were forecast. But these were 37.1 us of work at a share of 90%, and what came was 35.44 at 87%: both were forecast too high, and the quotient came out almost the same. In this profile H.1 was late by the load alone (1.82 us, the shift of lI.3 1.83).
- **From H.1 to the end of attention: right in sign, too small.** 3.5 us of idle time were to become 1.3 and became 0.
- **The front as a whole: near, by luck.** It came out at 1.1 us gained in the profiled execution; forecast were 0.9 (2.2 - 0.8 - 0.5). H.1 was 1.8 worse than forecast, the idle time 1.3 better, which leaves about 0.1 of the 0.8 for joints.
- **Behind endA: right up to u.0, and wrong there.** PE has no wait for a PSUM pair and no idle time before u.0. But new waits for PSUM pairs behind endA were named as a sign that the prediction is wrong, and the 1.24 us in u.0 are one.
- **Warm-up tile, alternation:** nothing against 0 shows; PE's busy time up to u.0 rose by 0.1 us.
- **Rival (1), "DVE sets the end",** had the right engine in the wrong stage: it was priced in attention, where DVE kept up.

The lower clock is no cause of the 3.5 us: the five runs of the changed kernel have mean granted clocks of 0.988 to 1.00, and the one at 1.00 was the slowest (566.5). Single executions may lose by it: in the six kernels with an execution at 0.984 or 0.985 (the two of the pieces aside) that execution is 1.3 to 2.9 us above the median of its kernel.
